# One order for four engines, and another set of resident weights, in a recurrent attention kernel

## The chip, the cores and the metric

The kernel runs on one core of a Trainium2 chip. Its time is the device time of one execution in microseconds; the median of several executions is compared. A profiled execution gives, besides its time, the record of every instruction and DMA packet.

## The reference

Four layers are applied to x (2048 rows of 640, bf16), each added to its input: A, B, A, B.

```python
x = x + A(layernorm(x), mem0, Wq, Wk, Wv, Wo)
x = x + B(layernorm(x), wqkv, wo)
x = x + A(layernorm(x), mem0, Wq, Wk, Wv, Wo)
x = x + B(layernorm(x), wqkv, wo)
```

A is a recurrent attention. It goes through x in 64 segments of 32 rows. To each segment it puts 8 memory rows in front, makes 40 rows, and computes attention with 32 heads of 192 over them (memory rows see everything, the others the rows up to their own). The output's first 8 rows are the next segment's memory, so segments follow each other strictly. B is a local attention with 32 heads of 20: each row attends to itself and to 7 earlier rows at distances 2, 4, ..., 14. The weights of A (Wq, Wk, Wv of 640 x 6144 and Wo of 6144 x 640) are the same in both A layers.

## The kernel before

Both A layers run in one pass. A step handles segment s of the first A layer and segment s - 2 of the second, 40 rows each, side by side as "l" = 0 and 1, so every weight is loaded into TensorE once for both (80 columns). The B layers of the segment before run in the same step, also for both. There are 66 steps with A and one last step with B alone.

The weights of A are cut into 64 halves of 480 KB (128 partitions x 1920 bf16): half 2i is Wk and 2i + 1 is Wq of pair i of heads, 32 to 47 are Wv, 48 to 63 are Wo. 32 of them stay in SBUF (RESIDENT). The others (STREAMED) are loaded again in every step into a ring of 5 slots, in two DMAs of 240 KB each, issued from SP (L250). SP issues a load as soon as the slot's last reader on TensorE, five streamed halves earlier, is done. In step 0 the streamed ones are also written to DRAM in the layout that later loads read (L247).

A step is a list of words, ORDER, and each word is a stage with a number. For the A layers: q (`qk`, 30 matmuls that project a pair of heads; ScalarE evicts to a ring of five QK tiles, L330), s (`scores` of 4 pairs, 32 matmuls; the softmax follows on VectorE and ScalarE, L350 to L363), t (`p_transpose`), va, vb (`v_seg`, values of two units of segment rows each), vc (`v_mem`, values of memory rows of four units), pv (probabilities by values), o (`o`, output projection, 15 matmuls into the accumulators acc). For the B layers: ln1 (`b_stats`), qkv (`b_qkv`: 75 matmuls, three evictions on ScalarE, L475; then the products of queries and keys, prod, half on VectorE and half on GpSimd, L480), logits (`b_logits`: 20 matmuls on prod, then the softmax up to attn), e (`b_expand`, five words, with a product and a sum on VectorE, L518 and L520), wo, ln2 (`beta_x`), store. input and alpha bring in new rows. `finish_step` takes the memory rows out of acc for the next step's ST.

PSUM has six buffers for all of these besides the two accumulators. The instructions of TensorE and SP stand in the order of the words (`manual_schedule(engines={PE, SP})`, L566). Those of VectorE, ScalarE and GpSimd are placed by the tile framework's scheduler. Every engine runs its own instructions in order.

## Time and profile before

| | before |
|---|---|
| median of 3 executions | 3635.21 us (3617.75 to 3640.99) |
| the profiled execution | 3648.06 us, span 3646.3 us |
| TensorE, matmuls | 3293.8 us busy (90%) |
| VectorE | 1994.9 us (55%) |
| ScalarE | 2084.7 us (57%) |
| GpSimd | 378.9 us (10%) |
| SP's DMA queue | 1060.00 MB, 88.4% of 16 DMA engines' time |
| mean granted TensorE clock | 0.982 |

Busy time is the union of an engine's instructions. Matmuls overlap in the array, so a busy TensorE is not one at its peak. The share of a DMA queue is the time that its packets took, over 16 engines. A wait is put down to what ended last before the waiting instruction. In the profile, PE is TensorE, PEld its weight loads, DVE VectorE, ACT ScalarE, POOL GpSimd, and L480 is line 480 of the kernel.

### The profile page before, as it was taken

Reading aid. Unit: us, or ns where it says so; the run is one execution under the profiler, and the core shown is the slowest. Engines: PE = TensorE matmul, PEld = TensorE weight load, DVE = VectorE, ACT = ScalarE, POOL = GpSimd, SP = SyncE. Lnnn points to the kernel's source line nnn. Section 1 sums busy time; section 2 is a strip of 40 time slices with the busy share of each in tenths; the row PEclk is TensorE's granted clock in tenths of the full one; section 3 lists DMA queues with packets and bytes.
Section 4 is the critical chain, followed back from the end, with each engine's and each line's share of the span. In section 5 each row is a group of like instructions: output and inputs, shape, how many; then the busy total and the mean of one; then the engine's idle time right before and its main releaser. Section 6 shows DMA issues by size and latency. Waiting matters only on the chain.

```text
span 3646.3 us, 185054 instructions
## 1 busy us (share of the span) xinstructions
PE 3293.8 (90%) x83325; PEld 2826.4 (78%) x83325; DVE 1994.9 (55%) x5057; ACT 2084.7 (57%) x4533; POOL 378.9 (10%) x467
## 2 busy tenths in 40 slices
PE   5789999999999999999999999999999989999997
PEld 3677787787878777777878777887778777778876
DVE  1346556555555655555565555556555555555554
ACT  2355665565655566565556556565666555655554
POOL 3110010110111001011100101110010110111000
PEclk7799999999999999999999999999999999999998
DMA  9989999898989999999999999999999988999995
GB/s 353 343 283 297 298 301 300 294 304 294 304 291 306 297 302 302 298 304 301 295 302 298 299 299 303 297 307 304 303 302 304 300 288 289 303 299 303 301 301 188
DMA packets 646218, 1090.19 MB, mean 299 GB/s; under 512 B 68648, under 2 KB 642736, under 8 KB 645424
## 3 DMA queue, kind: packets, MB, share of 16 engines
q1 hardware_dynamic: 640560, 1060.00, 88.4%
q8 instruction: 651, 10.67, 1.2%
q0 software_dynamic: 2560, 15.73, 1.1%
q10 hardware_dynamic: 2304, 2.62, 0.2%
q14 instruction: 143, 1.17, 0.1%
HBM read 1059.73 MB, written 18.35 MB: 296 GB/s over the span
## 4 chain that ended last, share of the span: by engine, by line
PE 56%; DMA 16%; DVE 11%; ACT 10%; issue 4%; SPq 3%; POOL 0%; ACTq 0%; POOLq 0%; DVEq 0%
PE qk_ps L328 18%; DMA wt<-Wr 12%; PE v_ps L385 9%; PE acc L428 8%; PE v_ps L398 5%; ACT V L389 3%; PE qkv_ps L473 3%; ACT V L402 3%; ACT QK L330 3%; PE s_ps L346 2%; PE o_ps L411 2%; DVE oT L520 2%; PE qk_ps L323 2%; PE s_ps L340 2%; SPq L250 2%
## 5 line engine op out<-in xcount | busy, mean ns | idle before, releaser
L330 ACT CAST QK<-qk_ps 128x480 bf16<-128x480 f32 x1056 | 578.6, 559 | 949.0 <-PE qk_ps L328 699.0
L328 PE MATMUL qk_ps<-ST,wt 128*128 128x80 bf16 x15840 | 718.8, 203 | 62.6 <-DMA wt<-Wr 45.1
L328 PEld LDWEIGHTS <-wt 128*128 128x128 bf16 x15840 | 628.4, 100 | 96.8 <-DMA wt<-Wr 64.9
L328 PE MATMUL qk_ps<-ST,res 128*128 128x80 bf16 x13860 | 625.4, 203 | 11.6 <-issue 6.0
L328 PEld LDWEIGHTS <-res 128*128 128x128 bf16 x13860 | 562.4, 101 | 39.8 <-issue 10.4
L389 ACT CAST V<-v_ps 64x384 bf16<-64x384 f32 x1056 | 495.8, 469 | 150.5 <-PE v_ps L385 131.4
L428 PE MATMUL acc<-ot,wt 128*128 128x80 bf16 x9900 | 498.4, 202 | 17.6 <-DMA wt<-in_A_Wo_dram 8.5
L402 ACT CAST V<-v_ps 32x384 bf16<-32x384 f32 x1056 | 494.7, 468 | 22.5 <-PE v_ps L398 3.2
L385 PE MATMUL v_ps<-res,ST 128*64 128x384 bf16 x3630 | 488.6, 331 | 13.0 <-DMA res<-in_A_Wv_dram 12.1
L428 PEld LDWEIGHTS <-wt 128*128 128x128 bf16 x9900 | 420.6, 100 | 33.0 <-issue 11.1
L414 ACT CAST ot<-o_ps 128x480 bf16<-128x480 f32 x528 | 269.3, 561 | 221.9 <-PE o_ps L411 220.6
L385 PEld LDWEIGHTS <-ST 128*64 128x64 bf16 x5280 | 286.5, 112 | 132.8 <-issue 26.5
L350 DVE TENSOR_TENSOR sb<-s_ps,maskA 128x320 f32<-128x320 f32 x264 | 129.1, 489 | 444.8 <-PE s_ps L346 444.8
L520 DVE TENSOR_REDUCE oT<-prod 128x64 bf16<-128x512 bf16 x330 | 337.6, 1024 | 8.9
L385 PE MATMUL v_ps<-wt,ST 128*64 128x384 bf16 x1650 | 320.1, 330 | 7.5 <-DMA wt<-in_A_Wv_dram 6.1
L428 PE MATMUL acc<-ot,res 128*128 128x80 bf16 x5940 | 300.6, 203 | 8.9 <-issue 5.6
L480 POOL TENSOR_TENSOR prod<-qT,kh 128x1280 bf16<-128x1280 bf16 x66 | 204.8, 3103 | 742.9 <-ACT kh L475 742.9
L428 PEld LDWEIGHTS <-res 128*128 128x128 bf16 x5940 | 251.4, 100 | 32.1 <-issue 28.1
L518 DVE TENSOR_TENSOR prod<-bc_ps,vh 128x512 bf16<-128x512 f32 x330 | 226.6, 687 | 79.4 <-PE bc_ps L515 79.4
L398 PE MATMUL v_ps<-res,ST 128*32 128x384 bf16 x3630 | 266.3, 331 | 0.0
L398 PE MATMUL v_ps<-wt,ST 128*32 128x384 bf16 x1650 | 264.5, 331 | 0.4 <-issue 0.4
L356 DVE TENSOR_REDUCE sm<-sb 128x8 f32<-128x320 f32 x264 | 128.3, 486 | 166.3 <-ACT sb L354 166.3
(121 smaller groups left out, 3960.7 us busy)
## 6 DMA issues: line engine op xcount, KB each, us to landing
wt<-Wr SPq DMA_DIRECT2D x4160, 240.0 KB, 4.6
Wr<-wt POOLq DMA_DIRECT2D x32, 480.0 KB, 6.6
wt<-in_A_Wq_dram SPq DMA_DIRECT2D x11, 480.0 KB, 9.4
res<-in_A_Wv_dram SPq DMA_DIRECT2D x11, 480.0 KB, 12.1
res<-in_A_Wk_dram SPq DMA_DIRECT2D x10, 480.0 KB, 9.7
wt<-in_A_Wo_dram SPq DMA_DIRECT2D x10, 480.0 KB, 9.7
wt<-in_A_Wk_dram SPq DMA_DIRECT2D x6, 480.0 KB, 8.7
res<-in_A_Wo_dram SPq DMA_DIRECT2D x6, 480.0 KB, 10.7
```

The source lines that it names most:

```text
L328: nc.tensor.matmul(ps[:, m, :, :], lhsT=w[m // 3][:, c, (m % 3) * P:(m % 3 + 1) * P], rhs=st[:, c, PAD:WIDE], start=(c == 0), stop=(c == N ...
L330: nc.scalar.copy(out=self.QK[i % NQK][:, 0:12 * LT].rearrange("p (m l t) -> p m l t", m=6, l=2), in_=ps[:, :, :, :].rearrange("p m t l -> ...
L350: nc.vector.tensor_tensor(out=sb[:, :, :], in0=sv, in1=self.maskA[:, :].unsqueeze(1).to_broadcast([P, 8, LT]), op=ALU.add)
L385: nc.tensor.matmul(ps[r:r + 64, :], lhsT=st[:, c, MID:WIDE], rhs=self.wv[j][:, c, :], start=(c == 0), stop=(c == NCH - 1), tile_position=( ...
L389: nc.scalar.copy(out=self.V[r:r + 64, j, :], in_=ps[r:r + 64, :])
L398: nc.tensor.matmul(ps[r:r + 32, :], lhsT=st[:, c, 0:MID], rhs=self.wv[j][:, c, :], start=(c == 0), stop=(c == NCH - 1), tile_position=(0, ...
L402: nc.scalar.copy(out=self.V[r:r + 32, j, :], in_=ps[r:r + 32, :])
L414: nc.scalar.copy(out=ot[:, :, :, :], in_=ps[:, :, :, :, :].rearrange("p j n l t -> p (j n) l t"))
L428: nc.tensor.matmul(a[:, at, :, :], lhsT=w[h][:, m, dc * P:(dc + 1) * P], rhs=self.ots[h // 2][:, 3 * (h % 2) + m, :, :], start=(h == 0 and ...
L480: eng.tensor_tensor(out=self.prod[:, :, l, :, :], in0=qT[:, :, l, :].unsqueeze(2).to_broadcast([P, NCH, BW, SEG]), in1=window(kh, l), op=A ...
L518: nc.vector.tensor_tensor(out=pv, in0=ps[:, :, :, :], in1=window1(self.vh, c), op=ALU.mult)
L520: nc.vector.tensor_reduce(out=self.oT[:, c, :].rearrange("p (l t) -> p l t", l=2), in_=pv.rearrange("p l w t -> p l t w"), op=ALU.add, axi ...
```

## The change

ORDER is replaced, STREAMED is replaced by another set of 32 halves, and the order of the words now also sets the order of VectorE's and ScalarE's instructions. For that, stages that use these engines twice, with a wait between, are split into words of their own: the scores' exponential (exp) and the rest of the softmax (soft); ln1 into sqr, stat, root, norm; ln2 into sqx, statx, rootx, normx; input into xs, xr, xn, xt; VectorE's half of the products of qkv (prod); logits into logits, explg, attn. GpSimd's half of prod stays in qkv. The two evictions of va3 go to VectorE. `finish_step` names its copies in another order. All instructions are the same otherwise, and each engine gets as many as before, but for va3.

```diff
+VECTOR = mybir.EngineType.DVE
+SCALAR = mybir.EngineType.Activation
...
 ORDER = """
-q0 q1 ln10 alpha0 q2 input0 q3 s0 va0 vb0 vc0 qkv0 q4 t0 q5 q6 q7
-s1 pv0 va1 vb1 vc1 logits0 q8 o0 q9 t1 o1 e0 q10 o2 e1 o3 q11
-s2 pv1 va2 vb2 vc2 e2 q12 o4 q13 e3 t2 q14 o5 e4 q15 wo0
-s3 pv2 va3 vb3 vc3 o6 o7 ln20 store0 t3 o8 o9 pv3 o10 o11 o12 o13 o14
+q0 q1 sqr0 q2 q3 stat0 q4 s0 root0 xs0 va0 exp0 xr0 norm0 xn0 q5 q6 q7 qkv0 soft0 prod0 vb0 logits0
+explg0 vc0 t0 q8 s1 pv0 va1 exp1 vb1 vc1 soft1 attn0 q9 q10 q11 t1 o0 o1 e0 s2 pv1 e1 o2 e2 o3 exp2
+o4 soft2 q12 e3 va2 vb2 vc2 q13 o5 e4 q14 q15 t2 wo0 o6 o7 s3 pv2 va3 exp3 vb3 soft3 vc3 o8 o9 sqx0
+t3 statx0 xt0 o10 pv3 o11 rootx0 store0 o12 o13 o14 normx0 alpha0
 """
...
-STREAMED = (1, 5, 6, 7, 8, 11, 13, 14, 15, 17, 22, 23, 25, 26, 29, 30, 31, 33, 35, 38, 41, 46, 48, 49, 50, 51, 53, 55, 56, 58, 60, 63)
+V_ON_VECTOR = (("va", 3),)
+STREAMED = (
+    1, 3, 5, 6, 8, 11, 12, 14, 16, 17, 18, 20, 23, 24, 27, 29, 30, 34, 35, 37, 40, 46, 49, 50, 51, 53, 54, 55, 56,
+    58, 59, 62,
+)
...
-        nc.scalar.activation(out=sb[:, :, :], in_=sb[:, :, :], func=ACT.Exp, scale=SCA)
+        self.sb[g] = sb
+
+    def exps(self, g):
+        self.nc.scalar.activation(out=self.sb[g][:, :, :], in_=self.sb[g][:, :, :], func=ACT.Exp, scale=SCA)
+
+    def soft(self, g):
+        nc = self.nc
+        sb = self.sb.pop(g)
         sm = self.w2.tile([P, 8], F32, name="sm")
...
+    def evict(self, what, g, out, in_):
+        if (what, g) in V_ON_VECTOR:
+            self.nc.vector.tensor_copy(out=out, in_=in_)
+        else:
+            self.nc.scalar.copy(out=out, in_=in_)
...
         self.prod = self.w1.tile([P, NCH, 2, BW, SEG], BF16, name="prod")
-        for l in range(2):
-            eng = nc.vector if l == 0 else nc.gpsimd
-            eng.tensor_tensor(out=self.prod[:, :, l, :, :], in0=qT[:, :, l, :].unsqueeze(2).to_broadcast([P, NCH, BW, SEG]),
-                              in1=window(kh, l), op=ALU.mult)
+        self.products(1, nc.gpsimd)
+
+    def products(self, l, engine):
+        engine.tensor_tensor(out=self.prod[:, :, l, :, :], in0=self.qT[:, :, l, :].unsqueeze(2).to_broadcast([P, NCH, BW, SEG]),
+                             in1=window(self.kh, l), op=ALU.mult)
...
-        with tc.manual_schedule(engines={PE, SP}):
+        with tc.manual_schedule(engines={PE, SP, VECTOR, SCALAR}):
```

More of the change, by code (lines that the diff above doesn't have):

```diff
@@ L58 @@
 ORDER = """
-q0 q1 ln10 alpha0 q2 input0 q3 s0 va0 vb0 vc0 qkv0 q4 t0 q5 q6 q7
-s1 pv0 va1 vb1 vc1 logits0 q8 o0 q9 t1 o1 e0 q10 o2 e1 o3 q11
-s2 pv1 va2 vb2 vc2 e2 q12 o4 q13 e3 t2 q14 o5 e4 q15 wo0
-s3 pv2 va3 vb3 vc3 o6 o7 ln20 store0 t3 o8 o9 pv3 o10 o11 o12 o13 o14
+q0 q1 sqr0 q2 q3 stat0 q4 s0 root0 xs0 va0 exp0 xr0 norm0 xn0 q5 q6 q7 qkv0 soft0 prod0 vb0 logits0
+explg0 vc0 t0 q8 s1 pv0 va1 exp1 vb1 vc1 soft1 attn0 q9 q10 q11 t1 o0 o1 e0 s2 pv1 e1 o2 e2 o3 exp2
+o4 soft2 q12 e3 va2 vb2 vc2 q13 o5 e4 q14 q15 t2 wo0 o6 o7 s3 pv2 va3 exp3 vb3 soft3 vc3 o8 o9 sqx0
+t3 statx0 xt0 o10 pv3 o11 rootx0 store0 o12 o13 o14 normx0 alpha0
 """
 def stages():
-    names = ("alpha", "ln1", "qkv", "logits", "input", "wo", "ln2", "store", "pv", "q", "s", "t", "va", "vb", "vc", "o", "e")
     plan = []
     for word in ORDER.split():
-        what = next(n for n in names if word.startswith(n) and word[len(n):].isdigit())
+        what = word.rstrip("0123456789")
         plan.append((what, int(word[len(what):])))
@@ L261, in input_load, with input_stats @@
         self.nc.sync.dma_start(out=self.x_sb[:, :], in_=self.x[t * P:(t + 1) * P, :])
-    def input_tile(self, t):
+    def input_stats(self, t):
         nc = self.nc
@@ L270, in input_tile, with input_root, input_norm @@
         nc.vector.bn_aggr(out=st[:, 0:2], in_=bst[:, :, :])
-        self.rsqrt(st[:, 1:2], st[:, 2:3])
+        self.x_st = st
+    def input_root(self, t):
+        self.rsqrt(self.x_st[:, 1:2], self.x_st[:, 2:3])
+    def input_norm(self, t):
+        nc = self.nc
+        x_sb, st = self.x_sb, self.x_st
         nc.vector.scalar_tensor_tensor(out=st[:, 3:4], in0=st[:, 0:1], scalar=-1.0, in1=st[:, 2:3], op0=ALU.mult, op1=ALU.mult)
@@ L274, in input_tile, with input_turn @@
         nc.vector.tensor_scalar(out=xn[:, :], in0=x_sb[:, :], scalar1=st[:, 2:3], scalar2=st[:, 3:4], op0=ALU.mult, op1=ALU.add)
+        self.x_n = xn
+    def input_turn(self, t):
+        nc = self.nc
+        x_sb, xn = self.x_sb, self.x_n
         xt = self.w1.tile([P, NCH, P], BF16, name="xnt"), self.w2.tile([P, NCH, P], BF16, name="xt")
@@ L287, in alpha_x, with ln_square @@
         self.nc.gpsimd.tensor_copy(out=tokens(self.ST[s % 2])[:, :, 0, NM:LT], in_=xt[0][:, :, o:o + SEG])
-    def ln_stats(self, src, n):
+    def ln_square(self, src, n):
         nc = self.nc
@@ L295, in ln_stats @@
         nc.vector.tensor_reduce(out=ssq[:, :], in_=sq[:, :, :].rearrange("p c n -> p n c"), op=ALU.add, axis=AX.X)
+        return ssq
+    def ln_stats(self, src, ssq, n):
+        nc = self.nc
         ps = self.ps.tile([P, 2, n], F32, name="ln_ps", tag="ps")
@@ L304, in ln_stats, with ln_apply @@
         nc.vector.scalar_tensor_tensor(out=r[:, :], in0=ps[:, 1, :], scalar=1.0 / D, in1=r[:, :], op0=ALU.mult, op1=ALU.subtract)
-        self.rsqrt(r[:, :], r[:, :])
-        return m, r
-    def ln_apply(self, src, m, r, dst, n):
-        nc = self.nc
         xc = self.w1.tile([P, NCH, n], F32, name="xc", tag="f32n")
         nc.vector.tensor_tensor(out=xc[:, :, :], in0=src, in1=m[:, :].unsqueeze(1).to_broadcast([P, NCH, n]), op=ALU.subtract)
-        nc.vector.tensor_tensor(out=dst, in0=xc[:, :, :], in1=r[:, :].unsqueeze(1).to_broadcast([P, NCH, n]), op=ALU.mult)
+        return xc, r
+    def ln_apply(self, xc, r, dst, n):
+        self.nc.vector.tensor_tensor(out=dst, in0=xc[:, :, :], in1=r[:, :].unsqueeze(1).to_broadcast([P, NCH, n]), op=ALU.mult)
     def qk(self, i):
@@ L353, in scores @@
         nc.vector.tensor_tensor(out=sb[:, :, :], in0=sb[:, :, :], in1=mx[:, :].unsqueeze(2).to_broadcast([P, 8, LT]), op=ALU.subtract)
-        nc.scalar.activation(out=sb[:, :, :], in_=sb[:, :, :], func=ACT.Exp, scale=SCA)
+        self.sb[g] = sb
+    def exps(self, g):
+        self.nc.scalar.activation(out=self.sb[g][:, :, :], in_=self.sb[g][:, :, :], func=ACT.Exp, scale=SCA)
+    def soft(self, g):
+        nc = self.nc
+        sb = self.sb.pop(g)
         sm = self.w2.tile([P, 8], F32, name="sm")
@@ L388, in v_seg @@
             r = SEG_ROW[j]
-            nc.scalar.copy(out=self.V[r:r + 64, j, :], in_=ps[r:r + 64, :])
+            self.evict(("va", "vb")[a], g, self.V[r:r + 64, j, :], ps[r:r + 64, :])
+    def evict(self, what, g, out, in_):
[3 more added lines that the diff above has]
+            self.nc.scalar.copy(out=out, in_=in_)
     def v_mem(self, g):
@@ L401, in v_mem @@
             r = MEM_ROW[j]
-            nc.scalar.copy(out=self.V[r:r + 32, j, :], in_=ps[r:r + 32, :])
+            self.evict("vc", g, self.V[r:r + 32, j, :], ps[r:r + 32, :])
     def pv(self, g):
@@ L433, in finish_step @@
         nxt = tokens(self.ST[(s + 1) % 2])
-        for a, cs in zip(self.acc, OUT_CHUNKS):
-            c = slice(cs[0], cs[-1] + 1)
-            if s + 1 == LAG:
-                nc.vector.tensor_copy(out=nxt[:, c, 0, 0:NM], in_=a[:, :, 0, 0:NM])
-            else:
-                nc.vector.tensor_copy(out=nxt[:, c, :, 0:NM], in_=a[:, :, :, 0:NM])
-        if s + 1 == LAG:
-            nc.gpsimd.tensor_copy(out=nxt[:, :, 1, 0:NM], in_=self.m0T[:, :, :])
         xr = self.w2.tile([P, NCH, 2, SEG], BF16, name="xr")
@@ L448, in finish_step, with rows_of_b, b_square, b_root @@
         rb = self.x2[:, :, :] if s >= LAG else self.zero[:, :, :]
-        for l, r in ((0, ra), (1, rb)):
-            for a, cs in zip(self.acc, OUT_CHUNKS):
-                c = slice(cs[0], cs[-1] + 1)
+        for a, cs in zip(self.acc, OUT_CHUNKS):
+            c = slice(cs[0], cs[-1] + 1)
+            if s + 1 == LAG:
+                nc.vector.tensor_copy(out=nxt[:, c, 0, 0:NM], in_=a[:, :, 0, 0:NM])
+            else:
+                nc.vector.tensor_copy(out=nxt[:, c, :, 0:NM], in_=a[:, :, :, 0:NM])
+            for l, r in ((0, ra), (1, rb)):
                 nc.vector.tensor_tensor(out=xr[:, c, l, :], in0=a[:, :, l, NM:LT], in1=r[:, c, :], op=ALU.add)
+        if s + 1 == LAG:
+            nc.gpsimd.tensor_copy(out=nxt[:, :, 1, 0:NM], in_=self.m0T[:, :, :])
         self.xr_next = xr
+    def rows_of_b(self):
+        return self.xr[:, :, :, :].rearrange("p c l t -> p c (l t)")
+    def b_square(self):
+        self.ssq_b = self.ln_square(self.rows_of_b(), 2 * SEG)
     def b_stats(self):
-        self.bs = self.ln_stats(self.xr[:, :, :, :].rearrange("p c l t -> p c (l t)"), 2 * SEG)
-        xn = self.w1.tile([P, NCH, 2 * SEG], BF16, name="xnB", tag="n")
-        self.ln_apply(self.xr[:, :, :, :].rearrange("p c l t -> p c (l t)"), *self.bs, xn[:, :, :], 2 * SEG)
-        self.xnB = xn
+        self.ln_b = self.ln_stats(self.rows_of_b(), self.ssq_b, 2 * SEG)
+    def b_root(self):
+        self.rsqrt(self.ln_b[1][:, :], self.ln_b[1][:, :])
+    def b_norm(self):
+        self.xnB = self.w1.tile([P, NCH, 2 * SEG], BF16, name="xnB", tag="n")
+        self.ln_apply(*self.ln_b, self.xnB[:, :, :], 2 * SEG)
     def b_qkv(self):
@@ L501, in b_logits, with b_exps, b_soft @@
         nc.vector.tensor_tensor(out=sb[:, :, :], in0=src, in1=mx[:, :].unsqueeze(1).to_broadcast([P, BW, hf]), op=ALU.subtract)
-        nc.scalar.activation(out=sb[:, :, :], in_=sb[:, :, :], func=ACT.Exp, scale=SCB)
+        self.sbb = sb
+    def b_exps(self):
+        self.nc.scalar.activation(out=self.sbb[:, :, :], in_=self.sbb[:, :, :], func=ACT.Exp, scale=SCB)
+    def b_soft(self):
+        nc, sb = self.nc, self.sbb
+        hf = SEG // 2
         sm = self.w1.tile([P, hf], F32, name="smb")
@@ L538, in b_wo, with beta_square, beta_stats, beta_root @@
             nc.vector.tensor_tensor(out=self.yT[:, :, o:o + SEG], in0=ps[:, :, 1, :], in1=self.xr[:, :, 1, :], op=ALU.add)
-    def beta_x(self):
-        if self.step > self.n_seg:
-            return
-        m, r = self.ln_stats(self.x2_next[:, :, :], SEG)
-        self.ln_apply(self.x2_next[:, :, :], m, r, tokens(self.ST[(self.step + 1) % 2])[:, :, 1, NM:LT], SEG)
+    def beta_square(self):
+        if self.step <= self.n_seg:
+            self.ssq_x = self.ln_square(self.x2_next[:, :, :], SEG)
+    def beta_stats(self):
+        if self.step <= self.n_seg:
+            self.ln_x = self.ln_stats(self.x2_next[:, :, :], self.ssq_x, SEG)
+    def beta_root(self):
+        if self.step <= self.n_seg:
+            self.rsqrt(self.ln_x[1][:, :], self.ln_x[1][:, :])
+    def beta_norm(self):
+        if self.step <= self.n_seg:
+            self.ln_apply(*self.ln_x, tokens(self.ST[(self.step + 1) % 2])[:, :, 1, NM:LT], SEG)
     def store(self):
@@ L561, in run @@
         nc, tc = self.nc, self.tc
-        self.resident, self.xt, self.wv, self.ots = {}, {}, {}, {}
+        self.resident, self.xt, self.wv, self.ots, self.sb = {}, {}, {}, {}, {}
         self.Wr = {h: self.dram.tile([P, HALF], BF16, name=f"Wr{h}") for h in range(N_HALVES) if h not in RESIDENT}
@@ L565, in run @@
         self.step = 0
-        with tc.manual_schedule(engines={PE, SP}):
+        with tc.manual_schedule(engines={PE, SP, VECTOR, SCALAR}):
             self.constants()
             self.input_load(0)
-            self.input_tile(0)
+            self.input_stats(0)
+            self.input_root(0)
+            self.input_norm(0)
+            self.input_turn(0)
             self.alpha_x(0)
             n_steps = self.n_seg + LAG
-            attend = {"q": self.qk, "s": self.scores, "t": self.p_transpose, "va": lambda g: self.v_seg(g, 0), "vb": lambda g: self.v_seg(g, 1), "vc": self.v_mem, "pv": self.pv, "o": self.o}
-            local = {"ln1": self.b_stats, "qkv": self.b_qkv, "logits": self.b_logits, "wo": self.b_wo, "ln2": self.beta_x, "store": self.store}
+            attend = {"q": self.qk, "s": self.scores, "exp": self.exps, "soft": self.soft, "t": self.p_transpose, "va": lambda g: self.v_seg(g, 0),
+                      "vb": lambda g: self.v_seg(g, 1), "vc": self.v_mem, "pv": self.pv, "o": self.o}
+            local = {"sqr": self.b_square, "stat": self.b_stats, "root": self.b_root, "norm": self.b_norm, "qkv": self.b_qkv,
+                     "prod": lambda: self.products(0, nc.vector), "logits": self.b_logits, "explg": self.b_exps, "attn": self.b_soft, "wo": self.b_wo,
+                     "sqx": self.beta_square, "statx": self.beta_stats, "rootx": self.beta_root, "normx": self.beta_norm, "store": self.store}
+            rows_in = {"xs": self.input_stats, "xr": self.input_root, "xn": self.input_norm, "xt": self.input_turn}
             for s in range(n_steps + 1):
@@ L593, in run @@
                         self.alpha_x(s + 1)
-                    elif what == "input" and s % 4 == 2 and 4 * (s // 4 + 1) < self.n_seg:
-                        self.input_tile(s // 4 + 1)
+                    elif what in rows_in and s % 4 == 2 and 4 * (s // 4 + 1) < self.n_seg:
+                        rows_in[what](s // 4 + 1)
                 if a:
```

## The prediction

> **What bounds the kernel now.** I read the engines' shares first, then the DMA queues and one stretch of the steady part, then the waits of TensorE's sequencer.

> ```profile
> PE 3293.8 (90%) x83325; PEld 2826.4 (78%) x83325; DVE 1994.9 (55%) x5057; ACT 2084.7 (57%) x4533; POOL 378.9 (10%) x467
> q1 hardware_dynamic: 640560, 1060.00, 88.4%
> wt<-Wr SPq DMA_DIRECT2D x4160, 240.0 KB, 4.6
> ```
> ```profile
> 2600.00:2700.00 100.00, 92.38 (x2390) 79.44 (x2387) 56.99 (x141) 58.10 (x126) 10.52 (x12) 1.00 0.93 307
> ```
> Two resources are nearly full together: TensorE is busy 92% and the 16 DMA engines 93%, at 307 GB/s. The streamed half-weights come in pieces of 240 KB that land 4.6 us after their issue. At a share of 1.0 the same row gives 307/0.93 = 330 GB/s; a step streams 32 halves, 64 pieces, 15.73 MB, so DMA alone needs at least 47.7 us of it.

> ```profile
> PEld L340 <- ACT QK L330: 96.1, 197, 0.8
> PEld L515 <- DVE attn L508: 85.8, 66, 3.2
> ...
> PEld L328 <- DMA wt<-Wr: 64.9, 134, 2.3
> PEld L428 <- issue: 39.2, 97, 2.1
> ```
> These are the waits of the weight loads (they share a sequencer with the matmuls, so one of the two is counted): each score word waits for the eviction of the projection just before it, the first expansion waits for the attention weights, and projections wait for the stream.

> To place this in the order I cut the matmul records of the trace into the words of ORDER (each word's count of matmuls is fixed) and took, for steps 8 to 64, the time from a word's first matmul to the next word's. A step takes 53.33 us on average. With each kind of word at its shortest unwaited time (q 1.07, s 0.63, va 0.82, vb 0.91, vc 0.93, pv 0.43, o 0.54, qkv 2.20, wo 0.83, logits 0.39, e and t 0.22) the step is 46.76 us. The other 6.6 us: 1.7 for QK evictions (0.53, 0.58 and 0.58 in s0, s1, s2; s3 has none), 1.3 before e0, 0.3 in wo0, 0.4 around t3 and pv3, 0.2 for the input and store words of every fourth step, 0.3 for changes between kinds of matmul, some 0.2 unplaced, and 2.2 for the stream and the step's start: q15 0.66, q7 0.24, q0 0.22, o14 0.21, q11 0.19, q3 0.14, the rest under 0.1 each.

> **The change, part by part.** No engine gets more or less work, except that two V evictions of each step go from ScalarE to VectorE. Everything turns on what is late where, so each TensorE word is set against its producer.

> *QK waits: minus 1.7 us a step.* Each score word now has other work between it and its last projection: stat0 and q4 before s0 (1.47 us), qkv0 to q8 before s1, t1 o0 o1 e0 before s2 (1.5 us). An eviction needs 0.25 us to start and 0.56 us to run. At s2 ScalarE is still behind (seven copies and an exponential, from pv0, va1, vb1, vc1, come before q11's), which leaves q11's copy about 0.1 us late for the fourth unit of s2; that goes into the small terms.

> *e0: minus 1.3 us.* Before, ScalarE and VectorE served V copies and s1 first. Now soft1 and attn0 stand before q9, and q9 to o1 are 4.5 us of matmuls. On VectorE attn0 (0.37 + 0.26 + 4 x 0.295 = 1.8 us) ends about 0.8 us ahead of e0.

> *logits0: plus 2.2 us, a new wait.* logits0 was behind q4 to vc1, some 9 us after qkv0; now only vb0 (0.91 us) lies between. Its third matmul needs the second half of prod, which GpSimd makes. The last step of the trace, where nothing stands between, shows what that costs:

> ```profile
> 3624.24 0.42 ACT L475 CAST kh<-qkv_ps 128x320 bf16<-128x320 f32 x1 [0.96 <-PE qkv_ps L473]
> 3624.70 0.83 DVE L480 TENSOR_TENSOR prod<-qT,kh 128x1280 bf16<-128x1280 bf16 x1 [3.43 <-ACT kh L475]
> 3624.74 3.10 POOL L480 TENSOR_TENSOR prod<-qT,kh 128x1280 bf16<-128x1280 bf16 x1 [6.99 <-ACT kh L475]
> ...
> 3625.58 0.23 PE L489 MATMUL lg_ps<-prod,E 128*32 128x128 bf16 x2
> 3627.89 0.46 PE L489 MATMUL lg_ps<-prod,E 128*32 128x128 bf16 x18 [2.08 <-POOL prod L480]
> ```
> In a step: kh's matmuls end 2/3 x 2.20 = 1.47 us after qkv0 begins; its copy starts 0.2 later and takes 0.43; GpSimd starts 0.08 later, runs 3.10, and TensorE follows 0.05 after: 5.33 us. TensorE is there after 2.20 + 0.91 + 0.03 = 3.14. It waits 2.2 us in every step. All that follows on TensorE (vc0, t0, q8, s1) stands behind it; VectorE's logits0 and ScalarE's explg0 wait too, and vc0's four copies queue behind explg0, which still ends about when vc0 does. SP is held as well: the slots of vb0's halves 34 and 35 come free only after vc0. GpSimd itself has nothing else ready there.

> *wo0, t3, pv3 and others: plus 0.1.* VectorE is nearly full between s1 and wo0: 17.9 us of work (s1, soft1, attn0, t1, five expansions of 0.69 + 1.02, s2, soft2, t2) and about 1.7 us in which soft1 waits for exp1 behind ScalarE's copies, beside 19.1 us of matmuls. e4 then ends a few tenths late; I keep wo0 at 0.3 and allow 0.2 for q14 waiting for e3's PSUM buffer. Before t3, va3's copies on VectorE have no row: the subtraction of 320 f32 takes 0.49, the product of 512 from PSUM 0.69, so 384 take 0.47 (ScalarE's time) to 0.69; with 0.55 each, soft3 ends 0.1 to 0.2 us late for t3, where before 0.4 was lost. The next step's start keeps its work: normx0 ends about half a microsecond ahead, and the copies of finish_step come in the order that VectorE already had.

> *Input and store words: nothing.* They are the same instructions; they lie beside matmuls. SP's load of x rows is issued at the same place, three steps after the last reader of its buffer.

> *The stream: plus 0.8, the uncertain term.* A streamed half is requested when the fifth before it is released. From the two orders, with the words' times and the waits above laid in, I listed the window from that release to the need. The mean falls from 7.05 to 6.78 us, as the step without stream waits gets shorter. Before, the tightest at words other than V are 4.42, 5.17 (q15), 5.53 (o14), 5.62 (q0), 5.64 (q7), 5.86 (q3). V words hardly waited though theirs are 5.6 and 5.95. The 2.2 us lost there are about the sum of what these lack to 5.7. After: 4.79 (q4), 4.94 (o7), 5.11 (q9), 5.46 (q3), 5.47 (o6), 5.50 (q0); they lack 2.9 to 3.0. The bounds: at a threshold of 5.0 the waits would fall by 0.3 and, with the refill during the 2.2 us pause, perhaps by 1.0; at 6.5 they would grow by 2.2.

> [...]

> **Sum.** Per step -1.7 - 1.3 + 2.2 + 0.1 + 0.8 = +0.1 us, times 65 steps +6 us. The first step (124 us, all 64 halves loaded once and 32 written back) and the last (a serial chain) move the same bytes and instructions: 0, give or take 5. On the profiled execution's 3648.06 us (span 3646.3) that gives about 3654; this execution is 13 us above the median of 3635.21, so the median comes to about 3641. I say 3640: no change that can be told. About 1% is what a measurement of this kernel can tell from none.

> **Rivals.**
> A, faster: the waits for the stream shrink. For it: the new list spreads streamed halves more evenly (three in a row at o1 to o3 instead of six from o0 to q11), and DMA refills four slots while TensorE waits for GpSimd. Against: the windows above. The terms without the stream are -0.7 a step; if the 2.2 us of stream waits fall to 1.0, that adds -1.2: -1.9, times 65 = -124, a median near 3510. Chance 0.26.
> B, slower: the ring of five slots decides. For it: DMA is at 0.93 already, and q0 to q7 use eight streamed halves in 9.35 us, 1.17 us each, where 480 KB at 330 GB/s takes 1.49. From the point where a typical half needs 6.5 us instead of 5.7, the waits grow by 2.2 instead of 0.8, +1.5 a step, +98: near 3735. Against: DMA's 2.2 us head start at the pause. Chance 0.32.
> C, GpSimd's product isn't late, so the change does what the order seems to mean: -2.1 a step, near 3505. Against: all 66 products took 3.10 us, and the built program keeps GpSimd's work and order as they were. Chance 0.02.
> My forecast, within 1%: 0.40.

> The range runs from between A and the forecast to B: 3545 to 3730; the forecast's own is 3605 to 3675. A and C give faster 0.28, B slower 0.32, the rest is within 1%.

> **What would show it.** Right: TensorE waits for GpSimd's prod at logits0 in 65 steps, some 2.2 us each (140 us), the waits on QK and attn go from 96 and 86 us to under 15 each, and stream waits grow by 30 to 70 us. Wrong: no such line of logits0, or stream waits that halve (A) or double (B).

## The result and the profile after

The changed kernel takes 3659.57 us (median of 15 runs, 3639.12 to 3681.25) against 3635.41 for the kernel before on the same chips (15 runs, 3617.75 to 3649.26). The ratio is 1.007, with a 95% interval of 1.0049 to 1.009: slower by 0.7%, within the 1% that was forecast as no change. The profiled execution took 3657.07 us, span 3655.2, mean granted clock 0.971 (0.982 before).

First the page of the changed kernel: busy time of the engines, SP's DMA queue, the shares of the chain that ended last, and the streamed pieces with their time to landing.

```profile
PE 3334.6 (91%) x83324; PEld 2847.2 (78%) x83325; DVE 2071.7 (57%) x5189; ACT 2069.8 (57%) x4401; POOL 378.5 (10%) x467
q1 hardware_dynamic: 640560, 1060.00, 86.1%
PE 65%; DMA 22%; POOL 6%; SPq 3%; issue 2%; ACT 1%; DVE 1%; POOLq 0%; ACTq 0%; DVEq 0%
wt<-Wr SPq DMA_DIRECT2D x4160, 240.0 KB, 4.9
```

The chain of the kernel before, for comparison:

```profile
PE 56%; DMA 16%; DVE 11%; ACT 10%; issue 4%; SPq 3%; POOL 0%; ACTq 0%; POOLq 0%; DVEq 0%
```

The chain shows the trade. VectorE and ScalarE had 11% and 10% of it before and now have 1% each; in their place stand GpSimd with 6% (it had none), 6 points more of DMA and 9 more of TensorE. TensorE is busy for 41 us more with the same matmuls, so some of them ran slower.

Next the waits of TensorE's weight loads in the changed kernel, and then its waits at matmuls (line waited for: total us, times, longest).

```profile
PEld L530 <- issue: 151.2, 131, 2.2
PEld L347 <- issue: 78.9, 229, 1.3
...
PEld L347 <- DMA wt<-Wr: 45.2, 106, 1.2
...
PEld L460 <- DMA wt<-Wr: 35.0, 69, 2.2
```
```profile
PE lg_ps L530 <- POOL prod L521: 122.3, 66, 2.0
PE qk_ps L347 <- DMA wt<-Wr: 28.6, 71, 1.1
PE acc L460 <- DMA wt<-Wr: 24.8, 58, 2.1
```

The two large rows of before, on QK (96.1 us) and on attn (85.8), are down to one wait of 0.6 and one of 3.2 us. In their place stands one row: logits0 (L530) waits in every step for GpSimd's half of prod.

The words' table (steps 8 to 64, each word's time above its shortest unwaited one, cut from the matmul records as in the prediction) gives a step of 53.54 us against 53.33. Of the 6.57 us above the unwaited 46.96, logits0 has 1.95, o7 0.48, q8 0.47, qkv0 0.28, vc0 0.26, q3 0.25, and no other word over 0.17.

One step in order of time: the timeline of the changed kernel from the eviction of kh to the next projection, other work left out (start us, duration, engine, line, operation, with the idle time before it in brackets).

```profile
1869.43 0.43 ACT L515 CAST kh<-qkv_ps 128x320 bf16<-128x320 f32 x1 [0.36 <-PE qkv_ps L513]
1869.89 0.83 DVE L521 TENSOR_TENSOR prod<-qT,kh 128x1280 bf16<-128x1280 bf16 x1 [3.48 <-ACT kh L515]
1869.94 3.09 POOL L521 TENSOR_TENSOR prod<-qT,kh 128x1280 bf16<-128x1280 bf16 x1 [13.64 <-ACT kh L515]
...
1870.94 0.23 PE L530 MATMUL lg_ps<-prod,E 128*32 128x128 bf16 x2
1873.09 0.72 PE L530 MATMUL lg_ps<-prod,E 128*32 128x128 bf16 x18 [1.92 <-POOL prod L521]
...
1873.49 0.53 PE L430 MATMUL v_ps<-res,ST 128*32 128x384 bf16 x1
...
1875.73 1.56 PE L347 MATMUL qk_ps<-ST,wt 128*128 128x80 bf16 x30
```

GpSimd's half ends at 1873.03, the third matmul of logits0 starts 0.06 later. Then comes something that the prediction doesn't have: the matmuls behind the pause last 0.53 us each, where the same line takes 0.33 in other steps, and the projection takes 1.56. The stretches of 3.41 us around this pause, in the changed kernel (busy us and counts of each engine, then granted clock, DMA share, GB/s):

```profile
1869.56:1872.97 3.41, 1.61 (x30) 0.97 (x27) 0.83 (x1) 1.67 (x4) 3.03 (x1) 1.00 0.58 213
1872.97:1876.38 3.41, 3.29 (x52) 2.46 (x52) 0.98 (x4) 1.19 (x3) 0.36 (x2) 0.50 0.02 5
1876.38:1879.80 3.42, 3.42 (x100) 2.83 (x97) 1.75 (x4) 3.05 (x7) 0.00 (x0) 0.99 0.97 291
```

The granted clock is 0.50 for one stretch and then back. This happens 30 times between 300 and 3400 us of the trace, and vc0, t0 or q8 is slow in 29 of the 57 steps from 8 to 64: in these steps vc0 takes 1.40 us and q8 1.91, in the others 0.96 and 1.17. The second row shows another thing: DMA moves 5 GB/s behind the pause. SP had issued its last load at 1868.00 and issues the next at 1875.43, right after vc0's last matmul, since the slots of vb0's halves come free only then, as the prediction has it.

### The profile page after: what moved, and what is told of

Read it like the earlier page. It is cut to its first block, busy times and chain, and to the rows that moved or that the text cites. A ratio compares the mean times of both kernels' runs of the same rounds, so it can differ in the third digit from the quotient of the medians.

```text
span 3655.2 us, 184659 instructions
## 1 busy us (share of the span) xinstructions
PE 3334.6 (91%) x83324; PEld 2847.2 (78%) x83325; DVE 2071.7 (57%) x5189; ACT 2069.8 (57%) x4401; POOL 378.5 (10%) x467
## 3 DMA queue, kind: packets, MB, share of 16 engines
q1 hardware_dynamic: 640560, 1060.00, 86.1%
q0 software_dynamic: 2560, 15.73, 1.1%
## 4 chain that ended last, share of the span: by engine, by line
PE 65%; DMA 22%; POOL 6%; SPq 3%; issue 2%; ACT 1%; DVE 1%; POOLq 0%; ACTq 0%; DVEq 0%
PE qk_ps L347 22%; DMA wt<-Wr 20%; PE acc L460 11%; PE v_ps L411 9%; PE v_ps L430 6%; POOL prod L521 6%; PE o_ps L443 3%; PE qkv_ps L513 3%; SPq L255 2%; PE s_ps L359 2%; PE s_ps L365 2%; PE pt_ps L396 2%; PE bc_ps L563 1%; PE qk_ps L342 1%; PE lg_ps L530 1%
## 5 line engine op out<-in xcount | busy, mean ns | idle before, releaser
L421 ACT CAST V<-v_ps 64x384 bf16<-64x384 f32 (+1 forms) x1980 | 920.4, 471 | 199.1 <-PE v_ps L411 147.6
L347 PE MATMUL qk_ps<-ST,wt 128*128 128x80 bf16 x15840 | 754.3, 206 | 52.9 <-DMA wt<-Wr 28.6
L347 PEld LDWEIGHTS <-wt 128*128 128x128 bf16 x15840 | 658.3, 103 | 95.4 <-DMA wt<-Wr 45.2
L347 PE MATMUL qk_ps<-ST,res 128*128 128x80 bf16 x13860 | 648.0, 203 | 15.9 <-DMA res<-in_A_Wq_dram 6.2
L460 PEld LDWEIGHTS <-wt 128*128 128x128 bf16 x9900 | 422.8, 101 | 84.7 <-DMA wt<-Wr 35.0
L411 PE MATMUL v_ps<-res,ST 128*64 128x384 bf16 x3630 | 432.0, 330 | 11.0 <-DMA res<-in_A_Wv_dram 7.8
L399 DVE TENSOR_SCALAR PT<-pt_ps,maskL 128x320 bf16<-128x320 bf16 x528 | 178.5, 380 | 219.7 <-PE pt_ps L396 219.5
L430 PE MATMUL v_ps<-res,ST 128*32 128x384 bf16 x3630 | 280.2, 339 | 0.0
L430 PE MATMUL v_ps<-wt,ST 128*32 128x384 bf16 x1650 | 279.5, 348 | 0.5 <-issue 0.5
L411 PE MATMUL v_ps<-wt,ST 128*64 128x384 bf16 x1650 | 266.0, 331 | 12.5 <-DMA wt<-in_A_Wv_dram 7.3
L430 PEld LDWEIGHTS <-ST 128*32 128x32 bf16 x5280 | 136.8, 99 | 101.5 <-issue 61.0
```

The source lines that it names most:

```text
L347: nc.tensor.matmul(ps[:, m, :, :], lhsT=w[m // 3][:, c, (m % 3) * P:(m % 3 + 1) * P], rhs=st[:, c, PAD:WIDE], start=(c == 0), stop=(c == N ...
L399: nc.vector.tensor_scalar(out=self.PT[g % 2][:, :, :, l, :], in0=ps[:, :, :, 0:LT], scalar1=self.maskL[:, l:l + 1], scalar2=None, op0=ALU. ...
L411: nc.tensor.matmul(ps[r:r + 64, :], lhsT=st[:, c, MID:WIDE], rhs=self.wv[j][:, c, :], start=(c == 0), stop=(c == NCH - 1), tile_position=( ...
L421: self.nc.scalar.copy(out=out, in_=in_)
L430: nc.tensor.matmul(ps[r:r + 32, :], lhsT=st[:, c, 0:MID], rhs=self.wv[j][:, c, :], start=(c == 0), stop=(c == NCH - 1), tile_position=(0, ...
L460: nc.tensor.matmul(a[:, at, :, :], lhsT=w[h][:, m, dc * P:(dc + 1) * P], rhs=self.ots[h // 2][:, 3 * (h % 2) + m, :, :], start=(h == 0 and ...
```

## The experiments

The theory after the result: the order itself saves time (the waits on QK, attn, wo0 and t3 go), and three things take it back, the wait for prod, a slow clock behind that wait, and more time lost to the stream. Rivals: the stream alone takes it back and the wait at logits0 would come up elsewhere if it went; or the resident set is the cause, not the order. "Unwaited" and "words' table" mean the same in all runs. Ratios are to the kernel before on the same chip, with 95% intervals; where there is none, the run is one execution.

### The stream switched off: changed kernel and kernel before

```diff
+        if self.step > 0:
+            kind = range(0, 32) if h < 32 else range(32, 48) if h < 48 else range(48, N_HALVES)
+            return self.resident[min((r for r in kind if r in RESIDENT), key=lambda r: abs(r - h))]
         t = self.ring.tile([P, HALF], BF16, name="wt")
```

A resident half stands in for each streamed one, so the output is not the reference's; only the time is of use.

> The changed kernel without the streamed loads after the first step: a resident half of the same kind is used in place of each streamed one, so what is left is the step without the stream. Theory 1 (stream waits of the changed kernel about 2.2 us a step, the rest wait and slow clock at logits0): a step of about 51.2 us, 3490 to 3520 in all. Theory 2, as in the prediction (stream waits 3.0 us, no loss by the clock): 50.4 us, 3440 to 3465.

> The kernel before without the streamed loads after the first step, as in the other run. If its stream waits are the 2.2 us a step that the words show: a step of 51.1 us, 3480 to 3505. If waits on other engines grow where the stream had covered them, up to 51.6 us, 3530.

Measured: 3501.37 us and 51.20 us a step for the changed kernel, 3544.07 and 51.82 for the one before. The first agrees with theory 1; the second is longer than the 3530 us allowed. Without the stream the change is a gain of 0.62 us a step, 43 us in all; with it a loss of 24. So the stream costs 2.34 us a step in the changed kernel (53.54 - 51.20) and 1.51 in the one before (53.33 - 51.82): 0.83 more. The wait at logits0 is still there (2.04) and so is the slow clock (q8 0.59, vc0 0.43), so neither comes from the stream. In the kernel before, wo0 goes from 0.31 to 0.86: the stream had hidden a wait there, which is why its loss looked like 2.2 in the prediction and is worth 1.5. The waits in the profile of the changed kernel without stream:

```profile
PE lg_ps L533 <- POOL prod L524: 127.0, 66, 2.1
```

### logits0 moved behind pv0

```diff
-... soft0 prod0 vb0 logits0
-explg0 vc0 t0 q8 s1 pv0 va1 ...
+... soft0 prod0 vb0
+vc0 t0 q8 s1 pv0 logits0 explg0 va1 ...
```

> The changed kernel with logits0 and explg0 moved behind pv0, so that GpSimd's 3.1 us product is done before TensorE needs it. Theory 1 (the wait at logits0, 1.95 us a step, and after it about 0.75 us a step in which the granted clock is 0.5): both vanish, 2.7 us a step gross; the stream gives 0.5 to 1.0 back, so 1.7 to 2.2 us x 65 = 110 to 145 us less than the changed kernel's 3660, some 3515 to 3550, and hardly any stretch of clock 0.5 after step 5. Rival (the ring decides): the pause at logits0 is when the stream catches up, so its removal turns into stream waits, and the time stays over 3620.

Measured: 3501.54 us, ratio 0.9622 (0.9597 to 0.9648); 51.08 us a step. This version beats both kernels, by 3.8% and 4.3%. From its profile, the engines, one stretch of the steady part, and the waits at matmuls:

```profile
PE 3295.8 (94%) x83325; PEld 2804.1 (80%) x83325; DVE 2065.3 (59%) x5189; ACT 2063.7 (59%) x4401; POOL 379.5 (11%) x467
```
```profile
2400.00:2600.00 200.00, 194.99 (x5014) 166.32 (x5011) 124.61 (x314) 123.81 (x264) 21.06 (x24) 1.00 0.94 317
```
```profile
PE qk_ps L347 <- DMA wt<-Wr: 30.8, 73, 1.7
PE acc L460 <- DMA wt<-Wr: 21.0, 55, 2.4
...
PE lg_ps L530 <- POOL prod L521: 2.0, 1, 2.0
```

The wait for prod is left in the last step alone, the slow stretches are 2 instead of 30, and TensorE's busy time falls by 39 us. No wait on VectorE or ScalarE took the place. The time is below the 3515 to 3550 expected; the next experiment shows why.

### The changed kernel with late logits, without the stream

> Two edits together: logits0 and explg0 stand behind pv0, and no half-weight is loaded after the first step (a resident half of the same kind stands in, so the numbers are not the reference's). The changed kernel without the stream took 51.20 us a step, of which 2.04 is the wait at logits0, 0.43 is vc0 above its unwaited time and some 0.49 is q8 above it (the clock at half speed behind the wait). If the wait, the slow clock and the stream are three costs that add up, a step takes 51.20 - 2.04 - 0.43 - 0.49 = 48.2 us and the kernel 3501 - 65 x 2.96 = about 3310 us; that also says that the stream still costs some 2.9 us a step in the order with the late logits (51.08 against 48.2). Rival: what the stream covers comes up as waits on other engines, as it did in the kernel before (wo0 0.31 to 0.86 without the stream): 3340 to 3380 us, with the waits at wo0, o1 or the score words over 0.4 us a step.

Measured: 3312.55 us and 48.23 us a step. The first theory's 3310 and 48.2 hold: the wait and its slow clock can be subtracted as they were measured. Its page (engines, queue, chain):

```profile
PE 3225.0 (97%) x83324; PEld 2780.5 (84%) x83325; DVE 2061.1 (62%) x5189; ACT 2055.7 (62%) x4401; POOL 378.7 (11%) x467
...
q1 hardware_dynamic: 41520, 37.37, 3.5%
...
PE 94%; DMA 3%; SPq 1%; DVE 1%; ACT 0%; issue 0%; POOLq 0%; POOL 0%; ACTq 0%; DVEq 0%
```

The chain is TensorE for 94% of its length: with this order little but the stream stands between the kernel and its matmuls. The stream costs 2.85 us a step there (51.08 - 48.23), against 2.34 in the changed kernel; and moving the two words gains 2.97 us without the stream (51.20 - 48.23) but 2.46 with it (53.54 - 51.08). It looks as if 0.5 went back to the stream, but the words' table says otherwise. In the table, pv0 is left out, as logits0 stands behind it in the late order:

| us a step, steps 8 to 64 | with stream | without | the stream costs |
|---|---|---|---|
| logits0, vc0, t0, q8, early logits | 5.39 | 5.79 | -0.40 |
| logits0, vc0, t0, q8, late logits | 2.84 | 2.72 | 0.12 |
| all other words, early logits | 47.70 | 44.97 | 2.73 |
| all other words, late logits | 47.70 | 44.97 | 2.73 |

In the other words the stream costs the same wherever logits0 stands. The difference lies in the pause and the words behind it, which are cheaper with the stream: 29 of the 57 steps have a slow stretch with it and 39 without; why there are more isn't shown. So 0.1 at most is a new wait for the stream, and the 0.5 to 1.0 that the late logits were expected to give back did not come.

### The wait without the slow clock, and more of both

In one kernel logits0 and explg0 stand behind vc0 (0.93 us later), in the other right behind qkv0 (0.91 us earlier).

```diff
 first kernel
-... vb0 logits0
-explg0 vc0 t0 ...
+... vb0 vc0
+logits0 explg0 t0 ...
 second kernel
-... soft0 prod0 vb0 logits0
-explg0 vc0 t0 ...
+... soft0 prod0 logits0
+explg0 vb0 vc0 t0 ...
```

The clock theory in both expectations is an estimate. In the changed kernel's trace the granted clock changes on a grid of 3.413 us, and the 30 slow stretches follow ones in which TensorE idled for 0.49 to 0.62 of the time; that half is always enough isn't shown, as 7 stretches of 0.50 to 0.56 had none behind them.

> The changed kernel with logits0 behind vc0 (0.93 us later): the wait for GpSimd's product is cut from 1.95 to about 1.1 us a step. Clock theory: the granted clock is set in fixed windows of 3.413 us, and one in which TensorE idles for half or more (1.7 us) is followed by one at 0.5; a wait of 1.1 us can't fill half a window, so fewer than 5 stretches of clock 0.5 are left between 300 and 3400 us. Minus 0.9 and minus 0.7 us a step, 0.4 given back to the stream: 3570 to 3590. Rival: any wait of about 1 us halves the clock; still 20 or more stretches, 3600 to 3625.

> The changed kernel with logits0 right behind qkv0, ahead of vb0: the wait for GpSimd's product grows from 1.95 to about 2.9 us a step. Clock theory: such a wait idles 1.7 us of one window of 3.413 us unless it is cut near its middle, so about 5 steps of 6 are followed by a stretch of clock 0.5, some 48 of 58 between 300 and 3400 us; plus 0.9 and plus 0.4 us a step, less 0.3 from the stream: 3710 to 3740. Rival (the length of the wait has no part): about 30 stretches again, 3690 to 3710.

Measured, behind vc0: 3541.68 us, ratio 0.9761 (0.9729 to 0.9793); logits0 waits 1.26 us a step, and there is no slow stretch at all; q8 is 0.10 above its unwaited time, vc0 under 0.04. Right behind qkv0: 3770.95 us, with 50 slow stretches; logits0 2.43 and qkv0 0.95 (which now holds the wait for VectorE's half, 0.67 a step), vb0 and vc0 0.55 each, q8 0.27. Their waits at logits0, first the kernel with logits0 behind vc0, then the other:

```profile
PE lg_ps L530 <- POOL prod L521: 69.2, 65, 2.1
```
```profile
PE lg_ps L530 <- POOL prod L521: 137.5, 66, 2.1
PE lg_ps L530 <- DVE prod L521: 44.2, 64, 0.7
```

So in these runs the slow clock came with the length of the pause and not with the wait as such: 1.26 us a step at logits0 brought no slow stretch, 1.95 brought 30 and 2.43 brought 50. In both kernels the time went further than I had said, down by 30 us and up by 30; the wait at logits0 fell by 0.7 in the first, the slow clock with it, and I haven't traced the rest beyond the words named here. Some 0.4 to 0.5 us a step in the first is made up of many words that fall by under 0.15 each.

### Both halves of prod on VectorE

```diff
-        self.products(1, nc.gpsimd)
-    "prod": lambda: self.products(0, nc.vector)
+    "prod": lambda: (self.products(0, nc.vector), self.products(1, nc.vector))
```

> The changed kernel with both halves of the product of queries and keys on VectorE (2 x 0.83 us) instead of one on GpSimd (3.10 us). Theory 1: the wait at logits0 falls from 1.95 to about 0.75 us a step, and so short a wait no longer halves the clock: minus 1.9 us a step gross, 0.5 given back to the stream, some 90 us less: 3550 to 3590. If the clock still halves: 3590 to 3620. Rival (the ring decides): over 3620.

Measured: 3526.65 us, ratio 0.9702 (0.967 to 0.9733), with 4 slow stretches; faster than the 3550 to 3590 expected, as the wait fell to 0.39 us a step and not to 0.75. The wait that is left, on VectorE:

```profile
PE lg_ps L529 <- DVE prod L520: 21.3, 61, 0.7
```

It undoes the cause by the other end: with the order kept, the product is whole after two instructions of 0.83 us instead of one of 3.09, some 1.4 us earlier. That the time falls by 133 us shows that the place of logits0 alone is not the price: it is GpSimd's duration at that place. It was less than moving logits0 brings, where no such wait is left.

### Each order with each resident set

```diff
 kernel before, set of the changed one
-STREAMED = (1, 5, 6, 7, 8, 11, 13, ...)
+STREAMED = (1, 3, 5, 6, 8, 11, 12, ...)
 changed kernel, set of the one before
-STREAMED = (1, 3, 5, 6, 8, 11, 12, ...)
+STREAMED = (1, 5, 6, 7, 8, 11, 13, ...)
```

> The kernel before with only the new set of streamed halves. By the windows between the release of a ring slot and the need of the next half, what they lack to 5.7 us grows from 2.2 to 3.8 us a step. Theory (the windows set the stream waits): plus 1 to 1.5 us a step, 3700 to 3735. Rival (the new set spreads the stream better in any order): 3600 or less.

> The order of the changed kernel with the resident set of the kernel before; with the kernel before, the changed one and the old order with the new set it completes a table of two orders by two sets. Theory 1, each set is fitted to its order, by the windows from a slot's release to its need: laid against the new order the old set's windows lack 11.7 us a step to 5.7 us, where the new set's lack 2.9; what is lost early moves the later windows too, so the waits for the stream grow by 3 to 5 us a step: 3850 to 3980 us. Rival, the set matters little in this order because transfers use the pause at logits0 to catch up: 3640 to 3700 us.

Measured: the old order with the new set 3756.93 us, ratio 1.0349 (1.0317 to 1.0381), more than the 3735 expected at most; the new order with the old set 3864.91, within what the first theory gave. In us a step, with the cost of the stream (the step less the same order's step without stream):

| | set of before | set of after |
|---|---|---|
| order of before | 53.33, stream 1.51 | 55.02, stream 3.20 |
| order of after | 56.67, stream 5.47 | 53.54, stream 2.34 |

Each set belongs to its order, as the first theory has it; either half of the change without the other is slower than the kernel before, by 3.5% and by 6.4%. With the new order and the old set the waits sit on a few projections, q7 with 1.42 us a step, q15 with 1.13 and q6 with 0.73, while DMA moves less (283 GB/s in the stretch below, 298 in the same stretch of the changed kernel). The waits at its matmuls, and then one stretch of its steady part:

```profile
PE qk_ps L344 <- DMA wt<-Wr: 160.5, 346, 2.2
PE lg_ps L527 <- POOL prod L518: 125.3, 66, 2.0
```
```profile
2400.00:2600.00 200.00, 178.52 (x4427) 152.46 (x4427) 107.63 (x278) 106.31 (x228) 17.33 (x21) 0.98 0.85 283
```

### A set chosen by the windows alone

The late logits, and a set of 32 halves chosen so that the shortest windows from a slot's release to its need are as long as could be found.

```diff
+STREAMED = (2, 3, 4, 6, 9, 11, 12, 14, 15, 16, 17, 20, 21, 23, 24, 25, 29, 30, 31, 34, 37, 38, 42, 46, 50, 51,
+    53, 55, 56, 57, 58, 60)
```

> The changed kernel with logits0 behind pv0, as in the faster run of this study (3501.5 us), and a set of streamed halves chosen so that what the windows between slot release and need lack to 5.7 us falls from 3.8 us a step to almost nothing. Theory (the windows set the stream waits): of the some 2.5 us of stream waits a step at least 1 us goes, 3410 to 3450. Rival (the DMA engines are full at the 312 GB/s of that run): no gain, 3490 or more.

Measured: 3530.65 us, ratio 0.9723 (0.9694 to 0.9751); 51.41 us a step. That is worse than the late logits with the planner's set (0.9622), where I had expected 50 to 90 us of gain. Its waits at matmuls and the same stretch as above:

```profile
PE qk_ps L347 <- DMA wt<-Wr: 67.3, 165, 1.7
...
PE acc L460 <- DMA wt<-Wr: 3.9, 10, 1.0
```
```profile
2400.00:2600.00 200.00, 193.68 (x4977) 165.15 (x4974) 123.24 (x313) 122.89 (x264) 20.75 (x23) 1.00 0.94 315
```

The window reading was right where it pointed: o7 falls from 0.49 to 0.10, and the waits in o almost vanish. They come up in q12 (0.59), q7 (0.54) and q15 (0.29), words whose two halves are both streamed, as q15, q7 and q11 are in the kernel before. But q1, q8 and q10 stream both halves here too and have only 0.13, 0.18 and 0.03. So the theory "a window under 5.7 us costs what it lacks" fails as a rule for choosing a set. Whether the pair has a part in it, or is merely the place where a DMA at 0.94 of its time shows its lack, stays open: DMA moves 317 and 315 GB/s in the stretches shown of the two.

## Why the prediction was right

The forecast's number held, 3640 against 3659.57 with a range of 3545 to 3730, and so did four of its terms. Two costs were wrong, with opposite signs and nearly the same size: it is right in part because they cancel.

| per step, us | foretold | measured |
|---|---|---|
| QK waits at s0, s1, s2 | -1.7 | -1.58 |
| attn at e0 | -1.3 | -1.29 |
| prod at logits0 | +2.2 | +1.95 |
| wo0, t3, pv3 and others | +0.1 | -0.67 (wo0 -0.41, o9 -0.26: it stood ahead of pv3 and now stands ahead of t3) |
| slow clock behind logits0 | not seen | about +0.65 (vc0 0.26, t0 0.09, q8 0.47 less the 0.17 of the late logits) |
| the stream | +0.8 | +0.7 in the words of the stream; +0.83 by switching it off |
| change between kinds of word | none | about +0.3 (e0, e3, o10, pv1, some 0.1 each) |
| sum | +0.1 | +0.21 by the step; the words above give about +0.1, the last 0.1 isn't placed |

**QK, e0, logits0.** Right in sign, place and nearly in size. The wait at logits0 is in the trace as it was worked out: kh's copy, GpSimd's 3.09 us behind it, TensorE 0.06 us later. The row was foretold as 140 us and is 122.3 at the matmuls and 151.2 at the weight loads, these with short gaps ahead of the first load.

**wo0 and t3: the term that had the wrong sign.** I had counted VectorE as nearly full between s1 and wo0 and put t2's evictions ahead of the last expansion. VectorE now follows the words, and t2 stands behind e4. In the changed kernel's timeline of VectorE around a wo0 that starts at 1368.09:

```profile
1366.72 1.04 DVE L568 TENSOR_REDUCE oT<-prod 128x64 bf16<-128x512 bf16 x1
1368.29 0.68 DVE L399 TENSOR_SCALAR PT<-pt_ps,maskL 128x320 bf16<-128x320 bf16 x2 [0.53 <-PE pt_ps L396]
```

The last sum ends at 1367.76, 0.33 us ahead, and t2's 0.68 comes after it: ahead of it, it would have made wo0 wait some 0.35, which is the 0.3 that was foretold. The 0.2 allowed for q14 did not come either (its excess is 0.01). At t3 the va3 copies took the 0.55 each that I had taken, and Pm ends at 1374.75, 0.45 ahead of t3 at 1375.20; why soft3 ends that much earlier than I had worked out isn't traced.

**The slow clock: a cost that was missing.** A wait on TensorE was priced at its own length. Here it costs about a third more on the average of all steps (0.65 us beside 1.95), and the addition falls in half of them (29 of 57).

**The stream.** The term of 0.8 lies between the two measures of it, of which the larger also counts the wait at wo0 that the stream had hidden in the kernel before. With the words left out in which other waits change with the stream (o1 and wo0 before, logits0, vc0, t0, q8 and pv0 after), it costs 2.16 us before and 2.73 after, 0.6 more. Its reading in the waits' view failed: there the weight loads' rows on streamed halves grow from 65.8 us to 81.6, by 16 and not by the foretold 30 to 70. Where the rest of it stands in that view I can't say; some is likely in the rows named "issue". The method behind the term agreed with the old order and the new set (a lack of 1.6 more, a step of 1.7 more), overshot on the new order and the old set (8.8 and 3.1) and failed on the set chosen by windows (3.8 less, 0.3 more), so its agreement here is no proof of it.

**The rivals.** A (the stream's waits shrink) and B (the ring decides) each had the stream term wrong; C (prod is not late) is out by the rows of logits0. What B named, that the stream grows as waits elsewhere go, isn't shown: the stream's cost of 1.51, 2.34 and 2.85 us a step seems to say so, but outside the pause it is 2.73 with the early and with the late logits, and the growth from the kernel before comes with another order and another set. (C's time was worked out wrong by a little: -2.1 times 65 from 3635 is 3499, not 3505.)

## What to carry to other kernels

When an order takes out waits on two engines, look up who else produces what the moved words need, and how long its instruction is: here a product of 3.1 us on GpSimd, whose reader was moved from some 9 us to 1 us behind qkv0, took back 2.6 of the 3.5 us a step that the order had gained, and moving two words of the order made the kernel 4.3% faster. Price a wait on TensorE together with what runs behind it: here a pause of 1.92 us was followed by 3.41 us at a granted clock of 0.50, and something is slow behind it in 29 of 57 steps. Where DMA is nearly full (0.93 of its time in the stretch that the prediction shows), an order and its resident set are one decision: test them crossed (here either half of the change alone was slower, by 3.5% and 6.4%). And when a gain is smaller with the stream than without it, compare the kernels word by word before the stream is blamed: here 0.4 of the 0.5 us lay in the pause and its slow clock.

## What was not expected of the hardware

```profile
1814.95:1818.36 3.41, 3.07 (x80) 2.42 (x77) 0.83 (x1) 2.12 (x5) 1.57 (x1) 1.00 0.62 201
1818.36:1821.77 3.41, 1.84 (x54) 1.48 (x54) 0.78 (x3) 1.08 (x4) 1.82 (x2) 1.00 0.42 139
1821.77:1825.18 3.41, 3.41 (x100) 2.77 (x96) 1.95 (x5) 3.31 (x8) 0.00 (x0) 1.00 0.79 234
```

TensorE is idle for 1.57 us of the middle stretch, 46%, and the clock stays at 1.00; in the step shown first it was idle for 1.80 of 3.41, 53%, and the next stretch ran at 0.50.
